# Moving two Relus, a split transpose, two dropped matmuls and a second DMA queue in a one-core convolution and MLP kernel

## The chip, the cores and the metric

The kernel runs on one core of one Trainium2 chip. The metric is the device time of one execution in microseconds (us); less is better. Three runs of the kernel before took 951.10, 953.44 and 954.62 us, so its median is 953.44 us. One more execution was profiled, and the profile and the trace come from that one. In what follows PE is the matrix engine (PEld its weight loads), DVE the vector engine, ACT the scalar engine, POOL is GpSimd and SP is SyncE, which here only issues DMAs. L523 is line 523 of the kernel before.

## What is computed

The input `x` has 8 sequences of 4224 rows of 192 numbers. A depthwise convolution along the sequence has 7 taps and 8 heads of 24 channels; its taps are a softmax of `weight`. Then comes a layer norm without bias, a hidden layer of 768 with Relu, and a residual sum:

```python
w = softmax(weight, axis=-1)                          # (8 heads, 7 taps)
y[b, s, h, :] = sum_k w[h, k] * x_pad[b, s + k, h, :] # 6 rows of zeros ahead
xn = (y - mean(y)) / sqrt(var(y) + 1e-6) * g_ln
out = y + maximum(xn @ w_ch1, 0) @ w_ch2
```

The weights arrive as float64 words, which the kernel takes apart and joins to float32 (`split_words`, `join_low`, `join_sign`, `join_product`). The centring and `g_ln` are folded into the first weight matrix (`centre_w1`), and the division by the standard deviation is applied to the output of the second product.

## The kernel before

**Groups.** Rows are worked in 18 groups, numbered g = 0 to 17. A group is a tile of 128 partitions with up to 16 rows each (J = 16) of 192 channels. Group 0 has 6 rows to a partition, group 1 gathers the tails of all 8 sequences (8 rows to a partition, 16 partitions to a sequence), group 2 has 10 rows; all others have 16. Groups 3 to 17 are "mixed": their products run as a seven-product scheme of Strassen's kind on quarters of the matrices, in `up_mixed` (first layer) and `down_fast` (second layer).

**Order.** The schedule is written by hand: each engine runs its instructions in the order of the program text, and semaphores tie the engines to each other. The eight banks of PSUM are taken in turn, in sets of four by `take_set`, so a product that wants a set waits until ACT has emptied what it held.

**The start.** SP loads the first weight matrix and x of group 0, and then the second weight matrix (L990) and x of group 1, which is 8 DMAs for 8 sequences (L142, inside `load_x(1)`). POOL's queue issues no DMA before L409. DVE convolves heads 0 to 4 of group 0 (L417). PE convolves heads 5 to 7 with diagonal matrices (`conv_on_pe`, L326), whose results ACT copies to `y` (L330). In between PE centres the first weight matrix and spreads it (`centre_w1`: L335, L340, and `copies_of_w1`: L354, L357), and ACT copies it out of PSUM (L362). `centre_w1` has a call `keep_warm(2)`, which issues two 128x128 matmuls into a bank that nobody reads (L367); each float32 matmul shows as two instructions. Then DVE transposes all of `y` of group 0 in one instruction (L428), and `up(0)` multiplies it with the first weight matrix in six steps, f = 0 to 5 (L533). ACT applies Relu and empties the banks (L523). Step f = 0 uses banks 0 to 3, f = 1 uses banks 4 to 7, then a `copies_of_w1` uses banks 0 to 3, and f = 2 wants banks 4 to 7 again. Between the Relus of f = 0 and f = 1 ACT runs four first taps of group 1 (L380), which read x of group 1.

**The mixed groups.** In `up_mixed` the lower right quarter of the hidden layer, `c22`, is closed by an adding DMA from the tile `parts_tb` (L617). Its larger part (pass `two`, two thirds of its blocks) then needs a Relu, in two halves (L675, 128x1024 each). These are not issued at once. They are put with others into the list `work`, which `down_fast` runs down on ACT behind its products: after every third (c = 0, 1, 2) of a product ACT copies a bank (L867) and then takes the next 3, 2, 2 or 3 entries of the list, for the first, second, third and fourth product. The list begins with a Relu of the smaller part of `c22`, the scaling of 14 rows of the previous group's output (L940; j = 2 to 15), the two Relus, and then first and second taps of group g + 2 (L380, L398). The third product reads `c22`: at c = 0 it takes the smaller part, then the first half, then the second half (`f in (PAIR, 0, 1)`).

```python
half = [lambda i=i: two.relu(two.c22[:, i : i + 1]) for i in range(PAIR)]
return work[0:9] + half + work[9:]
...
behind = (1, 1, 1, 1) if g == 2 else (3, 2, 2, 3)
```

Of the kernel before, what the change touches and what calls it, by code (L numbers as in the profile page):

```python
# [16 lines left out]
def kernel(  # L17
# [29 lines left out]
    nc = tc.nc  # L47
    PSUM = bass.MemoryType.PSUM
    B, S, D = x.shape
    H, K = weight.shape  # L50
    F = moe_w_ch1.shape[1]
    P = 128
# [9 lines left out]
    NC = D // C  # L62
# [23 lines left out]
    CH = NC // 2  # L86
# [33 lines left out]
    def take_bank():  # L120
        i = turn[0] % 8
        turn[0] = i + 1
        return all_banks[:, i]
# [9 lines left out]
    def load_x(g, queue=nc.sync, pad=True, gate=False):  # L133
        b, j0, n = groups[g]
        t = xpool.tile([P, J + PAD, D], F32, tag="xg", name=f"xg{g}")
        xg[g] = t
        flat = t.rearrange("p j d -> p (j d)")
        if gate:
            nc.vector.memset(t[0:1, 0:1, 0:1], 0.0)
        if b is None:  # L140
            for b in range(B):
                queue.dma_start(  # L142
                    out=flat[LP * b : LP * b + LP, 0 : (PAD + n) * D],
                    in_=bass.AP(
                        tensor=x.tensor, offset=(b * S + P * R - PAD) * D,
                        ap=[[n * D, LP], [1, (PAD + n) * D]],
                    ),
                )
            return
        if j0:  # L150
            queue.dma_start(
                out=flat[:, 0 : (n + PAD) * D], in_=xr[b, :, (j0 - PAD) * D : (j0 + n) * D]
            )
            return
        if b:

            queue.dma_start(
                out=flat[:, 0 : (PAD + n) * D],
                in_=bass.AP(
                    tensor=x.tensor, offset=(b * S - PAD) * D, ap=[[R * D, P], [1, (PAD + n) * D]]  # L160
                ),
            )
            if pad:
                nc.gpsimd.memset(t[0:1, 0:PAD, :], 0.0)
            return
        nc.gpsimd.memset(t[0:1, 0:PAD, :], 0.0)
        for p0, p1 in ((16, P), (1, 16)):
            nc.sync.dma_start(
                out=flat[p0:p1, 0 : (PAD + n) * D],
                in_=bass.AP(  # L170
                    tensor=x.tensor, offset=(b * S + p0 * R - PAD) * D,
                    ap=[[R * D, p1 - p0], [1, (PAD + n) * D]],
                ),
            )
        nc.sync.dma_start(out=flat[0:1, PAD * D : (PAD + n) * D], in_=xr[b, 0:1, 0 : n * D])
# [43 lines left out]
    for r in range(2):  # L219
        nc.sync.dma_start(  # L220
            out=raw1[Q * r : Q * r + Q, 2, :, :].rearrange("p f w -> p (f w)"),
            in_=w1_words[P:D, 2 * FH * r : 2 * FH * (r + 1)],
        )
    load_x(0)


# [90 lines left out]
    def tap_matrices(h, ks=range(K)):  # L317
        for k in ks:
            nc.scalar.mul(diag[:, h - PE_HEADS[0], k, :], unit, taps[:, h, k : k + 1])

    def conv_on_pe(h):
        n = groups[0][2]
        cs = slice(h * GRP, h * GRP + GRP)
        pc = take_bank()[:, 0 : n * GRP]
        for k in range(K):
            nc.tensor.matmul(  # L326
                pc, diag[:, h - PE_HEADS[0], k, :], xg[0][:, k : k + n, cs],
                start=(k == 0), stop=(k == K - 1),
            )
        nc.scalar.copy(y[0][:, 0:n, cs], pc.rearrange("p (j d) -> p j d", d=GRP))  # L330

    def centre_w1():
        pm = [take_bank()[:, 0:FH] for r in range(2)]
        for r in range(2):
            nc.tensor.matmul(pm[r], share[0], w1f[:, r, :], start=True, stop=False)  # L335
            if r == 0:
                keep_warm(2)
        conv_on_pe(PE_HEADS[2])
        for r in range(2):
            nc.tensor.matmul(pm[r], share[1 + r], w1f[:, 2, :], start=False, stop=True)  # L340
        tap_matrices(PE_HEADS[1], range(3))
        for r in range(2):
            nc.scalar.copy(mean[:, FH * r : FH * r + FH], pm[r])
        tap_matrices(PE_HEADS[1], range(3, K))
        conv_on_pe(PE_HEADS[0])
        copies_of_w1(0, [(q, 0) for q in range(NQ)])
        conv_on_pe(PE_HEADS[1])
        copies_of_w1(2, [(NQ, 0), (NQ + 1, 0), (NQ, 1), (NQ + 1, 1)])

    def copies_of_w1(s, parts):  # L350
        pw = [take_bank() for q in range(NQ)]
        for q in range(NQ):
            rows = slice(C * q, C * q + C)
            nc.tensor.matmul(pw[q][:, 0:FH], copy[rows], w1f[rows, s, :], start=True, stop=False)  # L354
        for q, (c, r) in enumerate(parts):
            rows = slice(C * q, C * q + C)
            nc.tensor.matmul(  # L357
                pw[q][:, 0:FH], less[rows], mean[rows, FH * r : FH * r + FH],
                start=False, stop=True,
            )  # L360
        for q, (c, r) in enumerate(parts):
            nc.scalar.copy(w1[:, c, FH * r : FH * r + FH], pw[q][:, 0:FH])  # L362

    def keep_warm(times):

        for _ in range(times):
            nc.tensor.matmul(idle[:, 0:P], less, less, start=True, stop=True)  # L367
# [54 lines left out]
    def transpose(g, c0=0, c1=NC):  # L422
        n = groups[g][2]
        if g == 1 and c0 == 0:
            yt[g] = yt[g - 1][:, groups[0][2] :]
        elif c0 == 0:
            yt[g] = tpool.tile([P, J, NC, C], F32, tag="yt", name=f"yt{g}")
        nc.vector.transpose(  # L428
            yt[g][:, 0:n, c0:c1].rearrange("p j c t -> p j (c t)"), y[g][:, 0:n, C * c0 : C * c1]
        )  # L430
# [188 lines left out]
    def up_mixed(g, ahead, pending):  # L619
# [170 lines left out]
        work = [lambda: one.relu(one.c22)]  # L790
        work += [lambda j=j: scale_one(j) for j in range(2, done)]
        half = [lambda i=i: two.relu(two.c22[:, i : i + 1]) for i in range(PAIR)]
        return work[0:9] + half + work[9:]

    def down_row(rows, left):

# [47 lines left out]
    def down_fast(g, work):  # L844
# [65 lines left out]
        if g + 1 < NG:  # L910
            sums_of_y(g + 1, nc.gpsimd)
            if g == 2:
                load_x(5, gate=True)
            moments(g + 1)
        else:
            finish_fast(g, 0, flat, cs, parts)
# [66 lines left out]
    for s in range(3):  # L983
# [7 lines left out]
        out=raw2.rearrange("p (c d) w -> p c (d w)", d=D),  # L991
        in_=w2_words.rearrange("(c p) d -> p c d", p=P),
    )
    load_x(1)
    tap_matrices(PE_HEADS[0], range(4))
    first_tap(0, heads=(0, PE_HEADS[0]))
    tap_matrices(PE_HEADS[0], range(4, K))
    conv(0, heads=(0, PE_HEADS[0]))
    centre_w1()
    transpose(0)  # L1000
    spare = cpool.tile([P, NC * NFAST * C], I32, tag="cs", name="spare")
    words_2 = (raw2, spare[:, 0 : NF * D], spare[:, NF * D : 2 * NF * D])
    split_words(*words_2, scaled=False)
# [3 lines left out]
    def ahead(g):  # L1007


        if results is not None:  # L1010
            for half in range(2):
                finish_fast(g - 1, half, *results)
        yield
# [3 lines left out]
    for g in range(NG):  # L1017
# [3 lines left out]
        if mixed:  # L1021
            work = up_mixed(g, ahead(g), pending)
            pending = iter(())
        else:
            up(g)
            work = []
# [90 lines left out]
```

## Time and profile before

| what | value |
|---|---|
| median of 3 runs (lowest, highest) | 953.44 us (951.10, 954.62) |
| profiled execution | 953.63 us |
| its span, first to last instruction | 951.4 us |
| PE busy | 944.5 us, 99% |
| DVE busy | 894.1 us, 94% |
| ACT busy | 700.0 us, 74% |
| POOL busy | 340.8 us, 36% |
| mean granted clock of PE | 0.999 |
| L861, the matmuls of `down_fast`, share of the chain that ended last | 34% |
| L533, the matmuls of the first layer, share of that chain | 32% |

The 2.2 us between the profiled execution's time and its span lie outside the first and the last instruction. A mixed group takes 55.0 us: 27.6 us of `up_mixed` and 27.4 us of `down_fast`. A line of a timeline gives the start and the length in us, then engine, line, operation, tiles written and read, shapes, the number of instructions merged into it, and in brackets how long the engine had been idle and what ended that. Matmuls are pipelined, so lengths of merged PE lines overlap: compare starts.

### The profile page before, as it was taken

What the parts mean: (1) busy time and instruction counts of PE and PEld (TensorE: products, weight loads), DVE (VectorE), ACT (ScalarE), POOL (GpSimd) and SP (SyncE); (2) the same over time, 40 slices, a digit from 0 to 9 for tenths busy, and PEclk for the clock granted to TensorE, in tenths of its full rate; (3) what the DMA queues carried; (4) which work ended last, traced back from release to release, by engine and by line L of the source; (5) the groups of instructions that cost most, each with busy time, mean ns of one, the idle gap of its engine ahead of it and who ended that gap; (6) DMA issues with size and microseconds to landing.
All of it is one profiled execution on the core that took longest, in us unless ns stands there. A gap on an engine that the chain in (4) does not pass through costs nothing.

```text
span 951.4 us, 38106 instructions
## 1 busy us (share of the span) xinstructions
PE 944.5 (99%) x16914; PEld 750.8 (79%) x16914; DVE 894.1 (94%) x1496; ACT 700.0 (74%) x1250; POOL 340.8 (36%) x474
## 2 busy tenths in 40 slices
PE   9999999999999999999999999999999999999998
PEld 7998896877859687787968778696877869586787
DVE  7999998999999999999999999999999999999867
ACT  6853678597877959787895968779696877967362
POOL 1158422723144142534218231452416332261330
PEclk9999999999999999999999999999999999999999
DMA  8359589689797887979697897979889797778261
GB/s 207 102 159 209 100 222 285 123 181 245 136 259 146 233 172 171 234 136 272 132 246 148 192 227 134 272 134 250 163 188 219 129 278 136 174 134 144 40 121 68
DMA packets 39834, 169.37 MB, mean 178 GB/s; under 512 B 4469, under 2 KB 8182, under 8 KB 33655
## 3 DMA queue, kind: packets, MB, share of 16 engines
q0 software_dynamic: 32864, 106.77, 60.5%
q1 hardware_dynamic: 6800, 60.16, 17.2%
q8 instruction: 133, 2.18, 0.9%
q14 instruction: 31, 0.25, 0.1%
q10 hardware_dynamic: 6, 0.00, 0.0%
HBM read 38.93 MB, written 50.33 MB: 94 GB/s over the span
## 4 chain that ended last, share of the span: by engine, by line
PE 67%; DVE 0%; issue 0%
PE ps L861 34%; PE ps L533 32%; PE ps L798 1%; DVE y L955 0%
## 5 line engine op out<-in xcount | busy, mean ns | idle before, releaser
L417 DVE SCALAR_TENSOR_TENSOR y<-xg,taps,y 128x384 f32<-128x384 f32 (+3 forms) x720 | 364.7, 582 | 3.3 <-DMA y<-tb 1.7
L861 PE MATMUL ps<-room,w2sums 128*32 128x256 f32 (+2 forms) x4608 | 246.9, 371 | 0.0
L533 PE MATMUL ps<-yt,w 32*128 32x256 f32 (+2 forms) x4160 | 237.9, 373 | 0.3 <-DVE yt L428 0.3
L533 PEld LDWEIGHTS ps<-yt,w 32*128 32x128 f32 x4160 | 211.0, 185 | 21.6 <-issue 6.2
L861 PEld LDWEIGHTS ps<-room,w2sums 128*32 128x32 f32 x4608 | 151.4, 110 | 89.5 <-ACT room L675 4.6
L662 ACT COPY room<-ps 128x512 f32<-128x512 f32 (+1 forms) x213 | 174.2, 859 | 62.6 <-PE ps L533 62.6
L861 PE MATMUL ps<-room,w 128*32 128x256 f32 (+2 forms) x3456 | 189.9, 371 | 0.4 <-DVE room L668 0.3
L828 DVE TENSOR_TENSOR room<-room 128x1024 f32<-128x1024 f32 (+2 forms) x147 | 161.2, 1170 | 22.4 <-PE ps L861 14.9
L861 PEld LDWEIGHTS ps<-room,w 128*32 128x32 f32 x3456 | 112.9, 110 | 69.3 <-DVE room L668 5.3
L533 PE MATMUL ps<-ysums,w1sums 32*128 32x256 f32 x2160 | 127.2, 376 | 0.3 <-issue 0.3
L533 PEld LDWEIGHTS ps<-ysums,w1sums 32*128 32x128 f32 x2160 | 116.5, 185 | 5.3 <-issue 0.7
L951 POOL DMA_DIRECT2D out_dram<-ot x69 | 59.0, 941 | 155.4 <-ACT ot L940 102.3
L409 POOL DMA_DIRECT2D y<-tb x59 | 52.5, 1386 | 154.5 <-ACT room L867 110.2
L867 ACT COPY cs<-ps 128x256 f32<-128x256 f32 (+2 forms) x192 | 70.0, 367 | 45.8 <-PE ps L861 45.8
L675 ACT ACTIVATE room<-room 128x1024 f32<-128x1024 f32 (+1 forms) x89 | 92.8, 1072 | 3.2 <-DMA room<-parts_cs 3.2
L940 ACT ACTIVATE ot<-ot,r 128x192 f32<-128x192 f32 x224 | 90.9, 464 | 0.0
L380 ACT ACTIVATE y<-xg,taps 128x384 f32<-128x384 f32 (+3 forms) x141 | 73.1, 608 | 0.4 <-DMA xg<-in_x_dram 0.4
L448 DVE BATCH_NORM_STATS2 st<-y 128x6 f32<-128x192 f32 x264 | 70.1, 344 | 0.0
L867 ACT COPY room<-ps 128x256 f32<-128x256 f32 (+2 forms) x96 | 35.5, 370 | 46.6 <-PE ps L861 44.9
L533 PE MATMUL ps<-yt,w1sums 32*128 32x256 f32 x1080 | 69.2, 375 | 0.0
L533 PE MATMUL ps<-ysums,w 32*128 32x256 f32 x1080 | 68.5, 374 | 0.0
L398 ACT ACTIVATE tb<-xg,taps 128x384 f32<-128x384 f32 (+1 forms) x120 | 66.1, 628 | 0.0
(119 smaller groups left out, 939.9 us busy)
## 6 DMA issues: line engine op xcount, KB each, us to landing
xg<-in_x_dram SPq DMA_DIRECT2D x14, 2112.0 KB, 16.2
room<-room POOLq DMA_DIRECT2D x45, 512.0 KB, 5.3
out_dram<-ot POOLq DMA_DIRECT2D x59, 384.0 KB, 9.6
y<-tb POOLq DMA_DIRECT2D x58, 384.0 KB, 8.8
out_dram<-y SPq DMA_DIRECT2D x13, 1536.0 KB, 9.1
room<-parts_cs POOLq DMA_DIRECT2D x28, 512.0 KB, 6.8
room<-parts_tb POOLq DMA_DIRECT2D x14, 1024.0 KB, 7.6
xg<-in_x_dram POOLq DMA_DIRECT2D x1, 2112.0 KB, 14.0
```

The lines of the kernel that those rows point to most:

```text
L380: nc.scalar.mul(y[g][:, 0:n, cs], xg[g][:, 0:n, cs], taps[:, h, 0:1])
L398: nc.scalar.mul(tb[g][:, 0:n, cs], xg[g][:, 1 : 1 + n, cs], taps[:, h, 1:2])
L417: nc.vector.scalar_tensor_tensor(out=y[g][:, 0:n, cs], in0=t[:, k : k + n, cs], scalar=taps[:, h, k : k + 1], in1=y[g][:, 0:n, cs], op0=AL ...
L448: nc.vector.bn_stats(out=sums[g][:, j, :], in_=y[g][:, j, :])
L533: nc.tensor.matmul(banks[:, q, i * w + j1 * t : i * w + j2 * t], right[rows, c, P * i : P * i + P], left[rows, j1:j2, c, :], start=start, ...
L662: nc.scalar.activation(to, of, AF.Relu) if relu else nc.scalar.copy(to, of)
L675: nc.scalar.activation(c, c, AF.Relu)
L828: nc.vector.tensor_tensor(a[:, *dst, f], a[:, *left, f], a[:, *right, f], op=op)
L861: nc.tensor.matmul(dst[C * q : C * q + C, 0:w], right[:, f, C * c : C * c + C], left[:, f, q], start=(first and f == PAIR), stop=(f == PAI ...
L867: nc.scalar.copy(to[:, c], dst[:, 0:w].rearrange("p (j t) -> p j t", t=t))
L940: nc.scalar.mul(ots[g][:, j, :], ots[g][:, j, :], rstd[g][:, j : j + 1])
L951: nc.gpsimd.dma_start(out=rows[:, d0:d1], in_=src[:, d0:d1], accum_op=ALU.add)
```

## The change

There are four edits. The text is the whole diff but for shifted line numbers.

1. `load_x(1)` becomes `load_x(1, gate=True)`: DVE first writes a zero into one element of each of the 128 partitions of the tile, and the DMAs wait for that. In program order this write stands behind DVE's last join of the first weight matrix. The 8 DMAs are shared: sequences 0 to 3 stay on SP's queue, 4 to 7 are issued by POOL.
2. `keep_warm(2)` in `centre_w1` is dropped.
3. The transpose of group 0 is made in two instructions, of channels 0 to 95 and of channels 96 to 191.
4. In the list `work` the two Relus stand two places further ahead, with a place that does nothing between them. The places are counted, so the entries behind come one place later.

```diff
         if gate:
-            nc.vector.memset(t[0:1, 0:1, 0:1], 0.0)
+            nc.vector.memset(t[0 : 1 if b is not None else P, 0:1, 0:1], 0.0)
         if b is None:
             for b in range(B):
-                queue.dma_start(
+                (queue if b < B // 2 else nc.gpsimd).dma_start(
...
             nc.tensor.matmul(pm[r], share[0], w1f[:, r, :], start=True, stop=False)
-            if r == 0:
-                keep_warm(2)
         conv_on_pe(PE_HEADS[2])
...
         half = [lambda i=i: two.relu(two.c22[:, i : i + 1]) for i in range(PAIR)]
-        return work[0:9] + half + work[9:]
+        return work[0:7] + [half[0], lambda: None, half[1]] + work[7:]
...
-    load_x(1)
+    load_x(1, gate=True)
...
     centre_w1()
-    transpose(0)
+    transpose(0, 0, CH)
+    transpose(0, CH, NC)
```

With the places counted out, ACT's order behind the third bank copy (c = 2) of the first product changes from "scale 7, 8, 9" to "scale 7, first Relu", and behind the first bank copy of the second product from "both Relus" to "second Relu, scale 8".

## The prediction

> **What bounds the kernel.** I read the page first, its busy shares and its chain.
>
> ```profile
> PE 944.5 (99%) x16914; PEld 750.8 (79%) x16914; DVE 894.1 (94%) x1496; ACT 700.0 (74%) x1250; POOL 340.8 (36%) x474
> ```
>
> PE is busy for 944.5 of 951.4 us and the chain that ended last is PE from 312.6 us on. PE's idle time is 6.9 us, 2.09 of it ahead of its first instruction. So no edit can win much: it must shorten what PE does, or close a gap in its stream. As lengths of pipelined matmuls hide small gaps, I compare starts in the timeline. All times below are from the span's start.
>
> The view of PE in the first 30 us shows the stretch that three of the four edits touch.
>
> ```profile
> 13.24 0.61 PE L367 MATMUL ps<-room 128*128 128x128 f32 x4
> 13.69 0.81 PE L335 MATMUL ps<-room 128*128 128x384 f32 x2
> ...
> 23.31 0.82 PE L357 MATMUL ps<-room 32*128 32x384 f32 x8
> 24.41 4.18 PE L533 MATMUL ps<-yt,w 32*128 32x192 f32 x96 [0.28 <-DVE yt L428]
> 28.42 0.82 PE L354 MATMUL ps<-room 32*128 32x384 f32 x8
> 29.06 0.82 PE L357 MATMUL ps<-room 32*128 32x384 f32 x8
> 29.71 8.03 PE L533 MATMUL ps<-yt,w 32*128 32x192 f32 x192
> ```
>
> Two losses stand there: the two dropped matmuls push the next one from 13.24 to 13.69, and the first product waits for the transpose. The same stretch on DVE says what the transpose itself waited for:
>
> ```profile
> 12.72 8.52 DVE L417 SCALAR_TENSOR_TENSOR y<-xg,taps,y 128x144 f32<-128x144 f32 x30 [0.17 <-ACT y L380]
> 22.98 1.38 DVE L428 STREAM_TRANSPOSE yt<-y 128x1152 f32<-128x1152 f32 x1 [1.74 <-ACT y L330]
> ```
>
> **Dropped matmuls.** The next matmul (L335) needs a join that ended at 10.95, so it can start at 13.24: 0.45 us earlier, and with it all that follows in order on PE. The convolution behind it reads x of group 0, and ACT read that x at 12.22. Bounds: nothing if such an input were late, 0.61 (the busy time) at most. I take 0.45, the distance of the starts.
>
> **Split transpose.** Channels 0 to 95 are heads 0 to 3, DVE's own, ready at 12.72 + 8.52 = 21.24. A transpose takes 0.98 us for 768 elements to a partition (at 38.83) and 1.38 for 1152, so about 0.78 for 576 by the straight line through both. The first half runs from 21.24 to 22.02, beside DVE's idle 1.74 us. The second waits as before for ACT's copy of head 6, which ended at 22.67 + 0.28 = 22.95 and now ends at 22.50: it is done at 23.3. PE's L357 needs 0.65 us to the next start (29.06 to 29.71), so without a wait the first product starts at 23.31 + 0.65 = 23.96, and with the 0.45 at 23.51. By then the transpose is over. PE is 0.90 us early here, 0.45 of it from this edit.
>
> **What is late next.** Step f = 2 of the product (29.71 before) wants the banks that step f = 1 filled, and ACT empties them in an unbroken chain:
>
> ```profile
> 24.15 1.63 ACT L362 COPY w<-ps 128x384 f32<-128x384 f32 x4 [1.20 <-PE ps L357]
> 25.64 1.20 ACT L234 ACTIVATE spare<-spare 128x1152 f32<-128x1152 int32 x1
> 26.71 0.82 ACT L523 ACTIVATE room<-ps 128x768 f32<-128x768 f32 x1
> 27.42 1.49 ACT L380 ACTIVATE y<-xg,taps 128x192 f32<-128x192 f32 x4
> 28.80 0.80 ACT L523 ACTIVATE room<-ps 128x768 f32<-128x768 f32 x1
> ```
>
> It ends at 29.60, 0.11 us ahead of PE's 29.71. Its head waits for L357, so it moves by 0.45 only, to 29.15. PE asks for the banks at 29.71 - 0.90 = 28.81 and gets them at about 29.2. Of 0.90 us some 0.50 is left, and that stays: behind it DVE and ACT moved by the same 0.45 or more, and PE ran there without a wait. **Early gain: 0.50 us** (bounds 0 and 0.90).
>
> **Gate and second queue.** The gate's write costs DVE 0.06 (the like memset L989 at 10.89) in the 0.17 it idles at 12.55. x of group 1 now starts at 12.6 instead of 11.45. SP needed 6.72 us for 8 issues; 4 are 3.4, to 16.0. POOL issued nothing from 5.7 to 45.10; its DMAs there show a price:
>
> ```profile
> 45.10 2.85 POOL L409 DMA_DIRECT2D y<-tb  x3 [39.40 <-ACT tb L398]
> ```
>
> 0.95 each, so four are issued by 16.4; the last of the 8 went out at about 17.9 before. Behind the waiting issues stand, on SP, the store of y at 22.97 and the next load at 23.45, and on POOL the work at 45.10: nobody is held. Nothing shows 16-partition loads from POOL's queue. Bounds to landing: 7.9 us (SP's pieces of the same 168 KB) and 14.0 (POOL's one load of 2112 KB), so 24.3 or 30.4. I take 24.3, the row of the same size. The first reader, ACT's L380, comes at 27.42 - 0.45 = 26.97: 2.7 us of cover, and cost zero. Past 26.97 each us of lateness is a us of PE, through the chain above.
>
> [...]
>
> **The Relus.** Timeline of a mixed group, ACT in its second-layer stage, which begins at 643.61:
>
> ```profile
> 648.70 0.37 ACT L867 COPY cs<-ps 128x256 f32<-128x256 f32 x1
> 648.96 1.15 ACT L940 ACTIVATE ot<-ot,r 128x192 f32<-128x192 f32 x3
> 650.01 0.37 ACT L867 COPY cs<-ps 128x256 f32<-128x256 f32 x1
> 650.26 2.02 ACT L675 ACTIVATE room<-room 128x1024 f32<-128x1024 f32 x2
> ```
>
> The Relus end at 652.28, and PE's weight load waits for that (0.36 idle at 652.33). What PE itself loses is seen from two pieces of 144 like matmuls, the first with the wait inside, the second without:
>
> ```profile
> 647.52 8.04 PE L861 MATMUL ps<-room,w2sums 128*32 128x256 f32 x144
> ...
> 659.26 7.95 PE L861 MATMUL ps<-room,w2sums 128*32 128x256 f32 x144
> ```
>
> 0.09 us. The list of waits has how often:
>
> ```profile
> PEld ps L861 <- ACT room L675: 4.6, 13, 0.4
> ```
>
> So the edit can give 13 x 0.09 = 1.17 us (14 groups run it; bound 1.26, and nothing). Does it? By starts, a copy costs ACT 0.26, a scaling 0.35, a Relu 0.95. New order: copy 648.70, scale 7 at 648.96, first Relu 649.31, copy 650.26, second Relu 650.52, which ends at 650.52 + 1.06 = 651.58. PE wants it at 652.33 - 0.09 = 652.24: 0.66 of slack. The copy that moved from 650.01 to 650.26 ends at 650.63 and is wanted when the third product starts, about 651.4 (two products of 3.9 after 643.61): 0.8 of slack. The copies behind come sooner, for one scaling and the empty place now stand behind them. Two scalings and their output DMAs come some 0.2 us later; that output tile is next written at about 673, 18 us on, and its DMAs take 9.6 us to land.
>
> The Relus need the adding DMA from `parts_tb`, issued at 640.70:
>
> ```profile
> DMA to landing us min/median/max: 4.9/7.6/8.7
> ```
>
> It lands at 648.3, at worst 649.4, for a Relu at 649.31. At worst 0.1 us is waited, inside the 0.66. I take 1.17 us.
>
> **Sum.** 0.50 + 1.17 = 1.67 us. The profiled execution goes from 953.63 to 951.96 (span 951.4 to 949.7), the median from 953.44 to **951.8**.
>
> **Rivals.**
>
> *No gain from the Relus.* PE's 0.09 may be spent elsewhere: something as late as the Relu, like the copy ahead of the third product, takes its place. For it: PE idles nowhere, so any slip shows. Against it: 0.66 and 0.8 of slack. Then only the early part is left, or, if ACT's chain or x takes that too, nothing: 952.9 to 953.4.
>
> *x of group 1 late (slower).* At the 14.0 of POOL's large load it lands at 30.4, 3.4 us behind ACT's L380; PE's step f = 2 slips by as much. 953.44 - 1.67 + 3.4 = 955.2. It decides from a landing at 26.97, and is slower than before from 28.6. For it: no row of such a load. Against it: 168 KB pieces took 7.9 us, and the DMAs have little else to do then.
>
> *The adding DMA late (slower).* A Relu that waits now holds back the copy behind it. From a landing 9.3 us after its issue each us costs 14. At 10.0 in every group 0.7 x 14 = 10 us: 961.6. For it: 8.7 was seen. Against it: no edit adds traffic there, and the old order had its limit at 9.5.
>
> **Chances.** Forecast 0.62; Relus without gain 0.24; x late 0.10; adding DMA late 0.04. 0.5% of the time, 4.8 us, is about what a measurement of this kernel can tell from no change. All gains at their bounds are 0.90 + 1.26 = 2.16 us, so faster by over 0.5% would need scatter: 0.02. Slower by over 0.5% is the last rival and a rest: 0.05. Within: 0.93. The range goes from all bounds with the runs' half spread of 1.8 (953.44 - 2.16 - 1.8 = 949.5) to the late x (955.2, with no more for scatter).
>
> **What would show it.** No L367 between the two L335, and L340 0.45 us earlier. The first L428 at 21.2 and no wait ahead of the first L533; a wait of f = 2 for ACT of about 0.35 us. No L675 among PEld's releasers, and 144 matmuls of the second and third product in 7.95 instead of 8.04. Wrong is the forecast if ACT's L380 at 27 waits for x, if L675 waits for `parts_tb`, or if the stages of 27.4 us keep their length.

## The result, and the profile after

Nine runs of the changed kernel have a median of 950.29 us (949.58 to 950.89), nine of the kernel before beside them 951.94 us (950.90 to 954.62). The ratio is 0.998 [0.9972, 0.9988], in medians 1.65 us less; 1.67 us were forecast. The nine also lie closer together, 1.3 us apart against 3.7. The absolute forecast, 951.8, stood on the three runs known then, whose median of 953.44 was 1.5 us above that of the nine. The profiled execution of the changed kernel took 949.91 us, with a span of 948.1: 3.3 us less span than in the profile of before.

First the list of waits; its columns are the total us, the number of waits, and the longest. `PEld ps L861 <- ACT room L675: 4.6, 13, 0.4` of before is gone: no line of PE's or of its weight loads names the moved Relus (now L673). The waits for DVE are there as before (`PEld ps L861 <- DVE room L668: 5.3, 15, 0.7`). One new line names ACT, and it belongs to the start:

```profile
PEld ps L859 <- DVE room L666: 5.0, 15, 0.3
PEld ps L531 <- ACT room L521: 0.8, 1, 0.8
```

The timeline of ACT and PE in a mixed group of the changed kernel shows why:

```profile
645.21 0.37 ACT L865 COPY cs<-ps 128x256 f32<-128x256 f32 x1
645.47 0.47 ACT L938 ACTIVATE ot<-ot,r 128x192 f32<-128x192 f32 x1
645.82 1.06 ACT L673 ACTIVATE room<-room 128x1024 f32<-128x1024 f32 x1
646.77 0.37 ACT L865 COPY cs<-ps 128x256 f32<-128x256 f32 x1
647.02 1.08 ACT L673 ACTIVATE room<-room 128x1024 f32<-128x1024 f32 x1
```

```profile
640.12 4.09 PE L859 MATMUL ps<-room,w 128*32 128x256 f32 x72
644.03 7.95 PE L859 MATMUL ps<-room,w2sums 128*32 128x256 f32 x144
...
655.68 7.95 PE L859 MATMUL ps<-room,w2sums 128*32 128x256 f32 x144
```

The second Relu ends at 648.10, and the piece of 144 matmuls that held the wait is as long as the one without: 7.95, not 8.04. In the chain of waits such a stage of 504 matmuls lasts 27.33 us where it lasted 27.42, here in before and then in the changed kernel:

```profile
643.68 27.42 PE ps L861 x504
```

```profile
612.58 27.61 PE ps L531 x504
640.19 27.33 PE ps L859 x504
```

The start of PE, against the timeline shown with the forecast:

```profile
7.35 3.39 PE L365 MATMUL ps<-room 128*128 128x128 f32 x28
10.58 1.79 PE L335 MATMUL ps<-room 128*128 128x384 f32 x4
12.88 1.95 PE L326 MATMUL ps<-xg,room 128*128 128x144 f32 x14 [0.51 <-DMA xg<-in_x_dram]
...
21.93 0.82 PE L355 MATMUL ps<-room 32*128 32x384 f32 x8
22.66 4.18 PE L531 MATMUL ps<-yt,w 32*128 32x192 f32 x96
26.64 0.85 PE L352 MATMUL ps<-room 32*128 32x384 f32 x8
27.28 0.85 PE L355 MATMUL ps<-room 32*128 32x384 f32 x8
28.28 3.04 PE L531 MATMUL ps<-yt,w 32*128 32x192 f32 x67
```

Step f = 2 begins at 28.28 instead of 29.71, but only part of this is the change's. The first line holds 28 idle matmuls, which both kernels issue and no edit touches. They took 5.02 us in the profile of before and 3.39 here: PE became fast (from 213 ns an idle matmul to 111) at 11.3 us there and by 7.6 here. The row of the granted clock shows 9, its highest digit, in every slice of both profiles, so only the matmuls' own spacing tells it. Comparing the two starts without looking at that line would credit the change with 1.43 us.

So of the 3.3 us between the spans, 13 x 0.09 = 1.17 are the Relus (of the 14 full second-layer stages one had no such wait before: it lasts 27.33 in both profiles), 1.43 the start, and most of the rest is stalls that the views call "issue" (the last section tells of them).

### The profile page after: what moved, and what is told of

Same layout as the page of the kernel before. It is cut to its first block, busy times and chain, and to the rows that moved or that the text cites. A ratio compares the mean times of both kernels' runs of the same rounds, so it can differ in the third digit from the quotient of the medians.

```text
span 948.1 us, 38092 instructions
## 1 busy us (share of the span) xinstructions
PE 940.8 (99%) x16910; PEld 751.7 (79%) x16910; DVE 893.7 (94%) x1498; ACT 699.8 (74%) x1250; POOL 342.7 (36%) x478
## 4 chain that ended last, share of the span: by engine, by line
PE 96%; DMA 2%; POOL 1%; ACT 1%; issue 0%; SPq 0%; DVE 0%; ACTq 0%; POOLq 0%
PE ps L531 46%; PE ps L859 44%; PE ps L796 4%; DMA xg<-in_x_dram 1%; DMA room<-room 1%; PE ps L326 1%; ACT room L660 0%; POOL room L615 0%; PE ps L352 0%; POOL d L458 0%; ACT w L360 0%; ACT room L521 0%; POOL r L481 0%; POOL d L476 0%; POOL d L477 0%
## 5 line engine op out<-in xcount | busy, mean ns | idle before, releaser
L415 DVE SCALAR_TENSOR_TENSOR y<-xg,taps,y 128x384 f32<-128x384 f32 (+3 forms) x720 | 364.2, 581 | 2.4 <-DMA y<-room 1.9
L859 PEld LDWEIGHTS ps<-room,w2sums 128*32 128x32 f32 x4608 | 154.7, 110 | 84.9 <-issue 0.8
L673 ACT ACTIVATE room<-room 128x1024 f32<-128x1024 f32 (+1 forms) x89 | 94.4, 1073 | 2.9 <-DMA room<-parts_cs 2.8
L938 ACT ACTIVATE ot<-ot,r 128x192 f32<-128x192 f32 x224 | 94.7, 468 | 0.0
```

The source lines that it names most:

```text
L415: nc.vector.scalar_tensor_tensor(out=y[g][:, 0:n, cs], in0=t[:, k : k + n, cs], scalar=taps[:, h, k : k + 1], in1=y[g][:, 0:n, cs], op0=AL ...
L673: nc.scalar.activation(c, c, AF.Relu)
L859: nc.tensor.matmul(dst[C * q : C * q + C, 0:w], right[:, f, C * c : C * c + C], left[:, f, q], start=(first and f == PAIR), stop=(f == PAI ...
L938: nc.scalar.mul(ots[g][:, j, :], ots[g][:, j, :], rstd[g][:, j : j + 1])
```

## The experiments

The theory: edit 4 gives 0.09 us in each mixed group, whatever else is done; edits 1 to 3 are worth about half a us at the start, capped by ACT's chain to f = 2. Rivals: the gain is the start's, with the Relus' gain spent elsewhere; or x of group 1, which edit 1 delays, takes the start's gain back. Unless a run says otherwise, every kernel computes the whole reference. In each comparison the kernel before has 23 to 35 runs, and each kernel 10 to 12 where nothing else is said.

**The Relus alone**: before, with edit 4.

```diff
-        return work[0:9] + half + work[9:]
+        return work[0:7] + [half[0], lambda: None, half[1]] + work[7:]
```

> The kernel before with the moved Relus alone (edit 4). Forecast's theory: each of 13 to 14 groups loses the 0.09 us that PE waited, so 1.1 to 1.25 us faster than before; in the profile the 144 matmuls of the second and third product take 7.95 us instead of 8.04 in every full group, and the start up to the first product is as before. Rival (the start alone made the gain, PE's 0.09 only moves elsewhere): within 0.3 us of before.

Measured: 951.96 us, ratio 1.0 [0.9989, 1.0011]. In its profile the stages are short, as the theory has it; the timeline shows the same pieces:

```profile
641.95 4.09 PE L861 MATMUL ps<-room,w 128*32 128x256 f32 x72
645.86 7.95 PE L861 MATMUL ps<-room,w2sums 128*32 128x256 f32 x144
```

But the time is that of before. The median of its spans is 0.6 us shorter (949.25 against 949.85), and in four of the twelve executions 2.8 to 3.1 us lie outside the span, where before has 2.1 to 2.3 in all 34. By time alone the theory fails here; by stages it stands. The run was made again, as **the Relus alone, repeated**:

> The kernel before with the moved Relus alone, a second time: in the first run every second-layer stage was 27.33 us instead of 27.42, which makes 1.2 us over 14 groups, but the time came out the same as before with an interval of 0.1% (1 us). If the 1.2 us are real and the scatter of the start and of PE's stalls hid them, the two runs together show 0.6 to 1.2 us. Rival (something outside those stages takes them back each time): again no difference.

Measured: 952.09 us, 0.9998 [0.9988, 1.0008]. The same again: the profile's stages at 27.33, spans 0.45 us shorter in the median, and 2.6 to 3.3 us outside the span in half of the executions. The forecast's 1.17 us would be a ratio of 0.9988, at the edge of both intervals: by time, a gain of that size is unlikely but not ruled out.

**The start alone**: the changed kernel with the old list.

```diff
-        return work[0:7] + [half[0], lambda: None, half[1]] + work[7:]
+        return work[0:9] + half + work[9:]
```

> The changed kernel with the Relus put back where they were (edits 1 to 3 alone). Forecast's theory: 0.5 us faster than before, in any run, because ACT's chain ahead of step f = 2 limits the start. Rival (the start's gain depends on when PE's matmuls become fast, 213 to 111 ns each, which fell at 11.1 us in the profile before and at 6.8 us in the profile after): f = 2 starts up to 1.4 us earlier than the 29.71 of before where that comes early, and about 0.5 us earlier where it comes late, so 0.3 to 1.4 us faster in the mean. The 8.04 us pieces of 144 matmuls stay.

Measured: 951.62 us, 0.9993 [0.9984, 1.0002], with spans as long as before's (949.80 against 949.85). Its stages are 27.42 again. The timeline of ACT shows a wait that the profile after didn't have, ahead of the first taps, for x of group 1 lands at 27.24 in the trace's DMA records; the label "issue" hides that. PE pays at f = 2:

```profile
26.06 0.84 ACT L521 ACTIVATE room<-ps 128x768 f32<-128x768 f32 x1
27.47 1.49 ACT L378 ACTIVATE y<-xg,taps 128x192 f32<-128x192 f32 x4 [0.57 <-issue]
```

```profile
23.40 4.18 PE L531 MATMUL ps<-yt,w 32*128 32x192 f32 x96
...
29.70 1.58 PE L531 MATMUL ps<-yt,w 32*128 32x192 f32 x32 [0.83 <-ACT room L521]
```

**The idle matmuls put back**: changed, without edit 2.

```diff
             nc.tensor.matmul(pm[r], share[0], w1f[:, r, :], start=True, stop=False)
+            if r == 0:
+                keep_warm(2)
```

> The changed kernel with the two idle matmuls put back. Forecast's theory: L326, and with it f = 2 and the time, come 0.45 us later than in the changed kernel. Rival: in the profile after PE waits 0.5 us for x of group 0 ahead of that convolution and the two matmuls (0.22 us once PE is fast) fit into that wait, so nothing changes unless PE becomes fast late; the kernel stays within 0.2 us of the changed one, which is 1.6 us faster than before.

Measured: 951.24 us, 0.9996 [0.9986, 1.0006]. Without the idle matmuls the same kernel stands at 0.998 [0.9972, 0.9988]: by the medians they cost about 1.5 us and not the forecast's 0.45, but the two intervals just overlap, so that more than 0.45 is likely and not shown. In its profile, where PE became fast late, L335 and the convolution behind it are 14.80 - 13.06 = 1.74 us apart, as in before; without the idle matmuls and equally late (next kernel) 14.34 - 13.05 = 1.29. That is the 0.45. It wouldn't explain a remainder.

**One transpose**: changed, without edit 3.

```diff
-    transpose(0, 0, CH)
-    transpose(0, CH, NC)
+    transpose(0)
```

> The changed kernel with the transpose of group 0 in one instruction. Forecast's theory: the first product starts 0.45 us later than with two halves, but f = 2 then finds its banks empty, so only 0.05 us (at most 0.35 us, the wait for ACT that f = 2 showed in the profile after) is lost in the time. Rival (the split gives its full 0.45 us): 0.45 us slower than the changed kernel.

Measured: 949.60 us, 0.9979 [0.997, 0.9987]: no slower than the changed kernel, so the split transpose gives nothing that can be measured, as forecast. The first product waits for the transpose, and f = 2 then waits for nobody:

```profile
24.42 4.18 PE L531 MATMUL ps<-yt,w 32*128 32x192 f32 x96 [0.28 <-DVE yt L426]
...
29.72 1.54 PE L531 MATMUL ps<-yt,w 32*128 32x192 f32 x32
```

With two halves this wait stands 5.3 us later, ahead of f = 2, and is put down to ACT. The time is the same.

**The changed kernel again**, beside the next two.

> The changed kernel once more, on the chip and beside the kernels of this call, as their yardstick: 1.6 us faster than before. Its start varies from execution to execution: x of group 1 landed at 24.0 us in the profile after, but at 27.2 and 27.5 us in two profiles of kernels with the same loads, where ACT's first taps waited for it or nearly. If it lands after ACT wants it (26 us), the taps wait and f = 2 starts about 2.4 us behind the landing.

Measured: 949.92 us, 0.9974 [0.9965, 0.9983]. PE was fast early, as in the profile after (28 idle matmuls in 3.39 us), but x of group 1 landed at 26.57 instead of 24.00, and f = 2 began at 29.03 instead of 28.28:

```profile
26.80 1.49 ACT L378 ACTIVATE y<-xg,taps 128x192 f32<-128x192 f32 x4 [0.31 <-issue]
```

```profile
29.03 2.23 PE L531 MATMUL ps<-yt,w 32*128 32x192 f32 x48 [0.56 <-ACT room L521]
```

**x of group 1 as before**: edits 2 to 4, x on SP's queue without the gate.

```diff
-                (queue if b < B // 2 else nc.gpsimd).dma_start(
+                queue.dma_start(
...
-    load_x(1, gate=True)
+    load_x(1)
```

> The changed kernel with x of group 1 loaded as before (edits 2 to 4: eight DMAs on SyncE's queue, no gate). Forecast's theory (edit 1 costs and gives nothing): within 0.2 us of the changed kernel. Rival (the gate delays x by 1.5 us and makes it late in some executions): x lands sooner, ACT's taps never wait for it, and the kernel is 0.3 to 0.8 us faster than the changed one. Other rival (second queue and gate are what brings x and x of group 0 in time): taps wait for x or L326 waits longer for x of group 0, 0.3 to 1 us slower than the changed one.

Measured: 950.62 us, 0.9981 [0.997, 0.9992]. Against the changed kernel's 0.9974 the intervals overlap: edit 1 is worth nothing that these runs resolve, in either direction.

**Two first taps later**: changed, and ACT runs only two of the four first taps ahead of the Relu of f = 1, the others behind it.

```diff
             if g == 0 and f == 0:
-                first_tap(1, heads=(0, H // 2))
+                first_tap(1, heads=(0, 2))
             elif g == 0 and f == 1:
+                first_tap(1, heads=(2, H // 2))
```

> The changed kernel with two of the four first taps of group 1 that stand between the Relus of f = 0 and f = 1 put behind the Relu of f = 1. If ACT's chain ahead of f = 2 is what takes back the split transpose's gain, as the forecast has it, f = 2 starts 0.35 us sooner after the last L355 (0.65 us behind it, as its banks are then empty in time) and the kernel is 0.3 us faster than the changed one, and more where x lands late. Rival (f = 2 waits for x or for PE alone): no change.

Measured: 949.21 us, 0.9968 [0.9957, 0.9979], the best of all medians; against the changed kernel beside it (0.9974) the intervals overlap. It takes 0.7 us out of ACT's chain. In the profiled execution x of group 1 was late again, at 27.20, and the chain waited for it:

```profile
24.42 0.83 ACT L521 ACTIVATE room<-ps 128x768 f32<-128x768 f32 x1
27.42 0.80 ACT L378 ACTIVATE y<-xg,taps 128x192 f32<-128x192 f32 x2 [2.17 <-DMA xg<-in_x_dram]
28.13 0.79 ACT L521 ACTIVATE room<-ps 128x768 f32<-128x768 f32 x1
```

Since a late x held the start, the next kernel loads it sooner. **x of group 1 ahead of the second weight matrix**:

```diff
+        if s == 0:
+            load_x(1, gate=True)
...
-    load_x(1, gate=True)
```

> The changed kernel with the gated load of x of group 1 put behind the join of the first third of the first weight matrix, so that it is issued some 3 us sooner (about 9.5 to 10 us) and ahead of the second weight matrix. If the landing of x rules the start where PE is fast early, as four profiles of the last two calls show (landing at 26.6 to 27.5, ACT's taps waiting 0.3 to 2.2 us), x lands by about 23, the taps no longer wait, f = 2 starts at 28.3 or sooner, and the kernel is 0.5 to 1 us faster than the changed one. Rivals: the second weight matrix then lands late and DVE's L233 (at 22 to 24) waits for it, or x of group 0 lands later, which takes it back: no change or slower.

Measured: 954.23 us, 1.0019 [1.001, 1.0028]: slower than before. x was in time; now the second weight matrix, behind it on SP's queue, landed 16.1 us after its issue. DVE waits for it, ACT for DVE, the Relu of f = 0 stands behind that on ACT, and PE gets its banks late. Three timelines, of DVE, ACT and PE:

```profile
27.47 0.76 DVE L233 TENSOR_SCALAR spare<-raw 128x1152 uint32<-128x1152 uint32 x1 [3.67 <-DMA raw<-in_moe_w_ch_dram]
```

```profile
28.27 1.16 ACT L234 ACTIVATE spare<-spare 128x1152 f32<-128x1152 int32 x1 [2.45 <-DVE spare L233]
29.34 0.79 ACT L521 ACTIVATE room<-ps 128x768 f32<-128x768 f32 x1
```

```profile
30.18 0.93 PE L352 MATMUL ps<-room 32*128 32x384 f32 x8 [2.10 <-ACT room L521]
30.93 0.82 PE L355 MATMUL ps<-room 32*128 32x384 f32 x8
32.25 5.00 PE L531 MATMUL ps<-yt,w 32*128 32x192 f32 x116 [0.50 <-ACT room L521]
```

f = 2 begins 4.0 us later than in the profile after, but PE was fast late here (28 idle matmuls in 5.51 us). Against one transpose and x as before, where PE was as late, it is 2.5 to 2.6 us, and that is the second weight matrix. By the ratios (1.0019 against 0.9974) the kernel is 4.3 us slower than the changed one, so some of that isn't accounted for.

**The same with the taps split and seven idle rounds instead of fourteen** (`keep_warm(14)` to `keep_warm(7)` at the start):

> The same with the first taps split around the Relu of f = 1, and seven instead of fourteen idle matmuls in the second call of keep_warm. The seven matmuls fewer let L335 start at about 11 instead of 12.6 to 13.1 us in executions where PE becomes fast late; f = 2 then starts at 27 to 28.5 in all. 1 to 2 us faster than the changed kernel, and the start scatters less. Rival (the idle matmuls are what makes PE fast, so that fewer of them keep it slow beyond 12 us): L335 and the first convolution take twice as long, up to 1.5 us lost.

Measured: 953.69 us, 1.0013 [1.0002, 1.0025]. The second weight matrix is the limit again (16.9 us to land, DVE's L233 at 28.55, f = 2 at 32.65). By time there is no verdict on the fewer idle rounds, for that limit hides them. But the trace shows half of the rival's sign. L335 came early, at 10.99; then PE waited for x of group 0 and ran the first convolution at 240 ns a matmul, twice the 122 of x sooner, so that it took 3.72 us instead of 1.88:

```profile
14.63 3.72 PE L326 MATMUL ps<-xg,room 128*128 128x144 f32 x14 [2.02 <-DMA xg<-in_x_dram]
```

The first product began at 26.09, 2.1 us later than in x sooner.

**The Relus four places further ahead**: changed, with another place in the list.

```diff
-        return work[0:7] + [half[0], lambda: None, half[1]] + work[7:]
+        return work[0:3] + [half[0], lambda: None, half[1]] + work[3:]
```

> The changed kernel with the two Relus four more places further ahead, behind the second bank copy of the first product. The slow rival of the forecast by its mechanism: the first Relu comes to 4.0 us behind the stage's begin, the adding DMA lands at 4.7 (7.6 after its issue), so ACT waits 0.7 us in each group, the bank copies behind the Relus come late, and the third product, which wants the copy at 7.8, gets it at about 8.3: the 27.33 us stages become 27.8 to 28.0 us, and the kernel is 7 to 9 us slower than the changed one. Rival (sooner is no worse): stages of 27.33 us, no change.

Measured (4 runs): 959.66 us, 1.0073 [1.0058, 1.0088]. The list of waits names the chain that the slow rival of the forecast described, a Relu waiting for the adding DMA and a bank copy behind it:

```profile
PEld ps L859 <- ACT cs L865: 13.4, 14, 2.0
...
ACT room L673 <- DMA room<-parts_tb: 9.5, 14, 1.7
...
PE ps L859 <- ACT cs L865: 6.6, 13, 1.5
```

The stages are 27.6 to 29.0 instead of 27.33, 27.95 in the middle. So edit 4's place is free and this one isn't: with the Relus two places ahead PE waits for nothing, with six places ahead it loses about 0.6 us a group. Where between them the limit lies, no run tells.

**The kernel before, profiled again**:

> The kernel before once more, for a second profile of it: its first profile, with 951.4 us, lies 1.6 us above the median span of its other executions. If the scatter is in the start and in PE's stalls, this one has an earlier first product of f = 2 (29.71 in the first) or fewer stalls (1.7 us over the stages in the first), while the second-layer stages are 27.42 us again.

Measured: 951.50 us, span 949.4. In this execution of before PE was fast early too, and f = 2 began as soon as in the earliest profiles of the other kernels:

```profile
6.77 3.39 PE L367 MATMUL ps<-room 128*128 128x128 f32 x28
...
22.89 4.18 PE L533 MATMUL ps<-yt,w 32*128 32x192 f32 x96 [1.03 <-DVE yt L428]
...
28.21 3.05 PE L533 MATMUL ps<-yt,w 32*128 32x192 f32 x68
```

28.21, against 28.28 in the changed kernel and 28.14 with the Relus further ahead: this pair shows no gain of the start. But the starts are not quite alike, for PE was fast from 5.6 us on here, and L335 began at 10.00 instead of 10.58. The stages of this profile are 27.42, as in the first.

## Why the prediction was right, and where it was not

The table puts the starts side by side, all from the traces' timelines and DMA records (us from the span's start). L335 is the first matmul behind the idle ones. In the first five PE became fast late, in the others early.

| kernel | 28 idle matmuls took | L335 began | x of group 1 landed | first product began | f = 2 began | from L335 to f = 2 |
|---|---|---|---|---|---|---|
| before | 5.02 | 12.60 | 24.68 | 24.41 | 29.71 | 17.11 |
| Relus alone | 5.17 | 12.73 | 26.36 | 24.55 | 29.84 | 17.11 |
| idle matmuls put back | 5.50 | 13.06 | 27.46 | 24.43 | 30.13 | 17.07 |
| one transpose | 5.48 | 13.05 | 25.94 | 24.42 | 29.72 | 16.67 |
| x as before | 5.43 | 13.00 | 26.90 | 23.92 | 29.62 | 16.62 |
| before again | 3.39 | 10.00 | 25.83 | 22.89 | 28.21 | 18.21 |
| Relus alone, repeated | 3.39 | 10.31 | 26.93 | 23.50 | 29.32 | 19.01 |
| changed | 3.39 | 10.58 | 24.00 | 22.66 | 28.28 | 17.70 |
| changed again | 3.39 | 10.48 | 26.57 | 22.99 | 29.03 | 18.55 |
| start alone | 3.39 | 10.83 | 27.24 | 23.40 | 29.70 | 18.87 |
| two first taps later | 3.39 | 10.69 | 27.20 | 21.76 | 28.97 | 18.28 |
| Relus four places further | 3.39 | 10.81 | 25.67 | 21.81 | 28.14 | 17.33 |

**The Relus: right, in mechanism and size.** 13 x 0.09 = 1.17 were forecast with 1.26 as the bound, and that came: the usual 27.42 became 27.33 in the profile of every kernel with edit 4 in its forecast place, and in none without it. The first profile of before had 13 of the waits, the second all 14, so it is 1.17 or 1.26 by the execution. No other wait took its place. That the shorter stages turn into time is seen only beside edit 2: the four kernels with edits 2 and 4 as forecast (changed, one transpose, x as before, two first taps later) stand at 0.9968 to 0.9981, those with one of the two edits at 0.9993 to 1.0.

**Dropped matmuls: the 0.45 is conditional.** The term is right where PE becomes fast late, as in the one profile it was read from (1.74 us became 1.29 between L335 and the convolution). Where PE is fast early, x of group 0 can end the wait there instead: 0.51 us at 12.88 in the profile after, 0.63 in the changed kernel again, 0.97 in the start alone, 0.39 even with the idle matmuls in the repeat of the Relus alone. With two first taps later and with the Relus four places further it was in time, and the distance was 1.29 and 1.30. The forecast took the moment when PE became fast (11.3 us) and the landing of x of group 0 in one execution for the kernel's.

**Split transpose: right.** Its own 0.45 is gone at f = 2, where ACT's chain is next, as forecast (with it, in x as before, the first product stands 10.92 behind L335 instead of 11.37, and f = 2 16.62 instead of 16.67); the predicted wait of about 0.35 us is 0.33 with x as before and with the idle matmuls put back.

**Gate and second queue: the landing was mis-sized.** The step that failed is "24.3, the row of the same size": the cover of 2.7 us isn't there. The last landing was 24.0, 25.7, 25.9, 26.6, 27.2, 27.2 and 27.5 in the seven profiles with the gate in this place, 7.2 to 13.1 us after an issue, nearly the whole width of the two bounds. The profile after met the 24.3 by luck: two terms were off and nearly cancelled. The last issue came at 15.0 and not at 16.4, for the four on SP took 1.97 us and not 3.4 (before, SP's eight took long because the last one stood 3.3 us apart) and the four on POOL 0.54 each and not 0.95; and it landed 9.0 us later, not 7.9. ACT's first taps began 0.3 to 2.2 us late in four of the seven, the forecast's own sign of being wrong, and f = 2 then waited 0.4 to 0.9 us for ACT; in all four PE was fast early and ACT there sooner. So the rival "x late" came true in the small, but not by the edit alone: the load without the gate landed at 24.7 to 26.9 in the five profiles that have it (read off the semaphore of its last DMA), and in the repeat of the Relus alone ACT's first taps began 0.47 us late for it and f = 2 waited 0.34. Gate and second queue hardly moved the landing, and none was as late as the 28.6 from which the forecast made the kernel slower. The four issues on POOL, from 13.34 us, stood beside DVE's L415 (13.31 us, 30 instructions in 8.52) and took 2.17 us in all:

```profile
13.34 2.17 POOL L142 DMA_DIRECT2D xg<-in_x_dram  x4 [7.64 <-DVE xg L139]
```

**The start's 0.50 together: there where PE is fast late, not seen where it is fast early.** In the table's first five rows x was in time, and from L335 to f = 2 it is 17.11 us in both kernels without edits 1 to 3 and 16.62 with edits 2 and 3: 0.49, where 0.50 were forecast. No late profile has all three edits. In the seven early ones ACT is ready for the first taps at 25.3 to 26.9 us, about when x lands, and in five of them the taps wait. There f = 2 began at 28.14 to 29.70 with edits 1 to 3 and at 28.21 and 29.32 without: the scatter of the landings is wider than the term. The median span of the start alone is that of before.

**That 1.65 was measured where the sum had 1.67 is luck**, then: the Relus gave 1.17 to 1.26, and the start 0.50 in some executions and nothing visible in others. Two terms that no step had make up for it, though no run isolates either. One is outside the span: 1.7 to 1.9 us in the changed kernel where before has 2.0 to 2.3, about 0.35 of the gain. The other is the first mixed group's first stage, 28.20 in the changed kernel against 28.42, at an "issue" stall:

```profile
120.97 1.02 PE L533 MATMUL ps<-ysums,w1sums 32*128 32x256 f32 x11
122.31 2.00 PE L533 MATMUL ps<-ysums,w1sums 32*128 32x256 f32 x32 [0.32 <-issue]
```

```profile
119.47 1.17 PE L531 MATMUL ps<-ysums,w1sums 32*128 32x256 f32 x15
120.81 2.21 PE L531 MATMUL ps<-ysums,w1sums 32*128 32x256 f32 x33 [0.17 <-issue]
```

The first fence is of before, the second of the changed kernel. 1.26 + 0.35 + 0.22 = 1.83, against a measured 1.65 and, in the repeat, 1.94. This is bookkeeping and no proof: in the start alone and in two first taps later the stall is absent and the same stage takes 27.93, and yet the start alone is no shorter in its span than before.

**Open.** Why edit 4 alone leaves the time unchanged in 24 runs, though its stages are shorter by 1.17 to 1.26 us, isn't settled: 0.45 to 0.6 us are seen in the median span, and in 10 of the 24 executions 0.4 to 1.2 us more lie outside the span, where the trace shows nothing. PE's stalls are as large as the gain, too. From the first mixed group's first matmul to the first of the last second-layer stage it is 800.47 and 799.84 us in the two profiles of before and 798.26 and 798.74 in those of the Relus alone, but also 798.51 in the start alone, which has the long stages and almost no stall. And the spans of the 24 executions reach from 947.7 to 951.4 us, so their median can't tell 0.5 from 1.26. Whether the two idle matmuls cost more than 0.45 beside edit 4 isn't settled either; their kernel, too, has 2.4 to 3.5 us outside the span in 4 of 11 executions. What causes either, no run shows.

## What to carry to other kernels

Where an engine is busy for 99%, read a wait by the length of the stage around it, against a like stage without it: 0.09 us, not the 0.36 us of idle weight load, and then count the stages. A start-up term from one profile holds for the moment when PE became fast and for the landings in that one execution; look how far they move in a second profile before adding it: here PE became fast at 5.6 to 12.3 us, and x of group 1 landed at 24.0 to 27.5. When a transfer is moved ahead of another, ask which of the two has the cover: with x sooner the second weight matrix, issued behind it, landed 16.1 us after its issue, and DVE waited 3.67 us for it. And compare two starts only where PE became fast at the same time, or from the first matmul behind that.

## What the runs showed of the hardware

- **When PE became fast differed by execution.** Idle 128x128 matmuls went from 213 to 111 ns at 5.6 to 7.8 us in seven profiles and at 11.3 to 12.3 in six, of kernels with the same idle matmuls up to there. (Small matmuls, L969 to L971 by the kernel, stand between the two rows of idle ones, from 6.2 us to 7.8 at the latest.) In two executions of the kernel before, PE became fast at 11.3 and at 5.6 us, and f = 2 began at 29.71 and at 28.21, 1.5 us apart. The idle matmuls began at 2.66, so PE became fast 2.9 to 9.6 us after that, at the upper end with those small matmuls in between.
- **PE was slow again behind a wait in one execution.** With seven idle rounds it was fast at L335 (323 ns a matmul from 11.5 us on, as in x sooner), waited 2.02 us, and needed 240 ns a matmul instead of 122 up to 18.0. Behind the wait of 0.97 us in the start alone it stayed at 122. One execution shows each.
- **One stall of PE sat at a fixed place in the instruction stream.** The stall at 121 us comes behind the 11th matmul of its piece in two profiles of before, at 121.99 and at 120.44 us by the clock, and behind the 15th in two profiles of the changed kernel, which has four matmuls less ahead of it: the same count from the program's start. Ten of the fourteen profiles have it at that count; the start alone, two first taps later, x sooner and the kernel with seven idle rounds haven't. Others come and go: one stands 361 matmuls into a stage near 440 us in the first profile of the changed kernel, in x as before and in two first taps later, but not in the changed kernel again. It makes that stage 0.56 us longer. No releaser is named there but "issue", and the profiles show no cause.
- **What lay outside the span differed between the kernels.** It is 1.7 to 1.9 us in every execution of the changed kernel, 2.0 to 2.3 in every one of before, of one transpose and of x as before, and from 1.7 to 3.5 in others.
- **The landing of one load was a range.** Of eight DMAs of 168 KB to 16 partitions each, the seven whose landing the trace ties to their issue took between 7.2 and 13.1 us in seven profiles of the same load.
